# First head pair of a causal attention: score matmuls over 128 rows, with zero rows below the queries, keys and sums

## The chip, the core and the metric

The kernel runs on one core of one Trainium2 chip, in one launch. The metric is the device time of that core in microseconds (us). A single profiled execution gives the rows below; the times of separate runs stand in the table further down.

## The reference, cut to what matters

Attention over 4 batches, 8 heads, 576 positions and a head size of 64, with a bias from running sums, feeds two feed-forward layers. Only the scores of the attention matter here:

```python
scores = scale * np.matmul(q, k.transpose(0, 1, 3, 2))
cum = np.cumsum(np.maximum(s, 0.0), axis=-1)
bias = -(cum[:, :, :, None] - cum[:, :, None, :])
scores = np.where(causal, -1000000000.0, scores + np.minimum(bias, 0.0))
scores = scores - np.max(scores, axis=-1, keepdims=True)
attn = np.exp(scores)
attn = attn / (np.sum(attn, axis=-1, keepdims=True) + 1e-09)
```

The running sum of the key's position is added to the score; the part of the bias that depends on the query alone drops out of the softmax.

## The kernel before, in words

TensorE makes all products. The attention works on head pairs, 16 in all; each head has five chunks of 128 queries (the last has 64). For a chunk, TensorE makes the scores (`ps_s`, L766), VectorE subtracts them from a mask and takes the row minimum (L781), ScalarE takes the exponent (L789), TensorE turns the result in pieces of 128 columns (`pt`, L811), ScalarE copies it out of PSUM (L354), and TensorE multiplies it with the values (`px`, L842 in the first batch). The last chunk's scores come in two pieces of 288 columns.

The order of each engine's instructions is fixed when the program is built: a small planner (`Flow`) hands engines to generators by rank and its own estimates of cost, and the program is emitted in that order. Meanwhile the feed-forward weights are decoded: a 512 KB block `raw` is loaded, ScalarE squares a half of it (L386), VectorE works on it (L388, L394, L399, L404), then it is split into two parts (L331, L335). The buffer of `raw` is free for the next load when L404 has read it. All loads are issued by SyncE's queue in its own fixed order (L308), and a load that waits holds up all behind it.

The first head pair (batch 0, pair 0) is made in another way than the other 15. Its queries and keys stay in plain float32, loaded straight into the tiles `qf` and `kf` (`qt`, `kt` in the profile) of `first_qk`, which are made in `setup` (L510 to L515). They have 128 partitions and 576 columns, of which 64 partitions hold data. For the first head (j = 0) there are two score passes (`first_head`, L586 to L595): queries against keys over 64 rows, and a column of the identity against the 32 rows of running sums (`c8`, `c` in the profile). For the second head (j = 1) there is one pass over 65 rows: `copy(first_qk[1][1][D:D + 1], c8[1:2])` at L566 writes the running sum of that head into row 64 of `kf`, and row 64 of `qf` is set to one at L514. The other 15 pairs use passes of 128 and of 66 rows at L766.

Ahead of all this, `setup` has TensorE multiply the identity by itself 20 times (`warm`, L527, two matmul records for each), while the first loads are under way.

The trace writes a matmul's stationary tile as rows*columns: "64*128 64x256" contracts over 64 rows, has 128 stationary columns and streams 256 columns. A float32 matmul shows as two records ("x2").

Of the kernel before, what the change touches and what calls it, by code (L numbers as in the profile page):

```python
# [20 lines left out]
B, H, S, D = 4, 8, 576, 64  # L21
# [235 lines left out]
def attn_moe_moe2(ctx, tc, q, k, v, s, w_in, w_out, w1, w2, w3, w_out2, out):  # L257
    nc = tc.nc
    vec, act, pool, pe, sp = nc.vector, nc.scalar, nc.gpsimd, nc.tensor, nc.sync
# [32 lines left out]
    ident = const.tile([P, P], F32, name="ident")  # L292
# [210 lines left out]
    def setup():  # L503
        make_identity(nc, ident)
        pool.memset(above, 0.0)
        pool.affine_select(
            out=above[:, 4 * P:], in_=above[:, 4 * P:], pattern=[[-1, P]],
            compare_op=ALU.is_ge, fill=MASK, base=0, channel_multiplier=1,
        )
        for x in range(2):  # L510
            qf, kf = (
                ap.tile([P, S], F32, tag=f"{t}{x}", name=t, bufs=1) for t in ("qt", "kt")
            )
            pool.memset(qf[D:D + 1], 1.0)  # L514
            first_qk.append((qf, kf))  # L515
        vec.memset(half, 0.5)
        for z in range(3):
            sums_of[z] = ap.tile([P, 2 * NCH], F32, tag=f"sums{z}", name="sums", bufs=1)
            vec.memset(sums_of[z], 1.0)
        e4 = ap.tile([P, NCH * P], F32, name="e4", bufs=1)  # L520
        pool.memset(e4[:S - 4 * P, S:], 0.0)
        et[0, "e4"] = e4
        et[0, 0] = ap.tile([P, 2, 2, 256], F32, tag="e1", name="e1p", bufs=1)
        et[0, 1] = ap.tile([P, 2, NCH, 320], F32, tag="e2", name="e2p", bufs=1)
        warm = psa.tile([P, P], F32, tag="t0", name="warm", bufs=1)
        for n in range(WARM):
            pe.matmul(warm, lhsT=ident, rhs=ident, start=(n == 0), stop=(n == WARM - 1))  # L527
# [58 lines left out]
    def first_head(h, j, qf, kf, dq, dk):  # L586
        yield dq
        yield dk
        c8 = yield first_cum[j]
        if j == 0:  # L590
            h.ready.set([
                (qf[0:D], kf[0:D]), (ident[0:B * H, 0:1].to_broadcast([B * H, S]), c8),
            ])
        else:
            h.ready.set([(qf[0:D + 1], kf[0:D + 1])])  # L595

    def lend_decoder():
        for f in range(NA):
# [23 lines left out]
    def prepare(x):  # L622
        b, p = pairs[x]
        pr = pair[b, p]
        if x == 0:
            for j in range(2):
                r = slice(j * D, (j + 1) * D)
                h = heads[b, p, j]
                qf, kf = first_qk[j]
                dq = yield from load(qf[0:D], q[b, p][r], 4 * D * S)  # L630
                dk = yield from load(kf[0:D], k[b, p][r], 4 * D * S)
                h.release = [(QK, (yield QK.get()))]
                flow.start(flow.cur.prio, first_head(h, j, qf, kf, dq, dk))
            loaded[b, p].set()
            flow.start(flow.cur.prio, values_in(b, p))
            return
# [959 lines left out]
    def late_weights():  # L1596
        yield heads[WO_AFTER].ready
        for f in range(NA):
            flow.start(WO_PRIO + WO_STEP * f, decode(w_out[f], W, ("o", f)))

    setup()
    flow.start(-20, cumulate())
    flow.start(0, issue_pairs())
# [71 lines left out]
```

## Time and profile before

| | us |
|---|---|
| median of three runs | 930.67 |
| the runs | 930.1, 930.67, 937.26 |
| the profiled execution | 932.69 |
| its span, first to last instruction | 930.9 |

TensorE is busy for 912.9 us of the span, VectorE for 708.0, ScalarE for 480.6 and GpSimd for 191.6. The span lies 1.8 us under the profiled execution's own time. The granted clock of TensorE is given as a share of full speed: 1.00 is 2.4 GHz and 0.50 is 1.2 GHz; its mean over the span is 0.981.

### The profile page before, as it was taken

The page shows a single profiled execution, that of the slowest core. Times are in us where ns is not written, and L with a number is a line of the kernel's source. Part 1 is how long each engine was busy: PE and PEld are TensorE (multiplying, and loading weights), DVE is VectorE, ACT ScalarE, POOL GpSimd, SP SyncE. Part 2 cuts the span into 40 slices and gives each one's busy share as a digit, 9 for nine tenths or more (in the row PEclk, how much of TensorE's full clock was granted, in tenths as well). Part 3 has the DMA queues.
Part 4 walks back from the last instruction along what each step waited for, and adds up shares of the span by engine and source line. Part 5 has one row for each costly group of instructions (what it writes and reads, how often), then busy time and mean ns, then how long its engine had stood idle before and what let it go on. Part 6 is the DMA issues. An engine that isn't in the chain of part 4 may idle for free.

```text
span 930.9 us, 18684 instructions
## 1 busy us (share of the span) xinstructions
PE 912.9 (98%) x6532; PEld 856.4 (92%) x6532; DVE 708.0 (76%) x1816; ACT 480.6 (52%) x1216; POOL 191.6 (21%) x242
## 2 busy tenths in 40 slices
PE   9989799999999999999999999999999999999998
PEld 5545599999999999999999999999999999999998
DVE  5658978787878629998685899985858576677994
ACT  3667667787777635564453455543323232333552
POOL 4546865546543123300000000000000000000000
PEclk7899899999999999999999999999999999999999
DMA  6799977688776145664658587948752120283542
GB/s 185 195 258 252 256 220 208 178 244 229 200 199 177 48 150 167 219 206 145 192 183 299 168 302 262 347 178 323 243 184 65 63 66 33 85 300 103 165 142 77
DMA packets 97269, 174.93 MB, mean 188 GB/s; under 512 B 10620, under 2 KB 59772, under 8 KB 97176
## 3 DMA queue, kind: packets, MB, share of 16 engines
q1 hardware_dynamic: 97176, 173.75, 60.9%
q8 instruction: 52, 0.85, 0.4%
q14 instruction: 41, 0.34, 0.1%
HBM read 97.99 MB, written 49.17 MB: 158 GB/s over the span
## 4 chain that ended last, share of the span: by engine, by line
PE 84%; DVE 7%; DMA 5%; issue 1%; ACT 1%; SPq 1%; POOL 0%; DVEq 0%; POOLq 0%; ACTq 0%
PE ps_s L766 7%; PE ps_j L433 7%; PE ps_j L434 7%; PE ps_j L435 7%; PE ps_h L433 6%; PE ps_x L433 6%; PE ps_x L435 6%; PE ps_x L434 6%; PE ps_h L434 6%; PE ps_h L435 6%; PE pt L811 5%; PE px L849 5%; PE ps_o L434 2%; PE ps_o L435 2%; PE ps_o L433 2%; PE px L842 2%
## 5 line engine op out<-in xcount | busy, mean ns | idle before, releaser
L433 PE MATMUL ps_h<-x,w 128*128 128x288 f32 x512 | 155.3, 303 | 0.0
L433 PE MATMUL ps_x<-gt,w 128*128 128x288 f32 x512 | 153.0, 299 | 1.2 <-DVE g L978 1.2
L434 PE MATMUL ps_h<-x,w 128*128 128x288 f32 x512 | 151.2, 295 | 0.0
L435 PE MATMUL ps_x<-gt,w 128*128 128x288 f32 x512 | 151.2, 295 | 0.0
L435 PE MATMUL ps_h<-x,w 128*128 128x288 f32 x512 | 150.7, 294 | 0.0
L434 PE MATMUL ps_x<-gt,w 128*128 128x288 f32 x512 | 150.5, 294 | 0.2 <-DVE gt L335 0.2
L434 PE MATMUL ps_j<-xf,wf 128*128 128x288 f32 x432 | 127.9, 296 | 0.0
L433 PE MATMUL ps_j<-xf,wf 128*128 128x288 f32 x432 | 127.8, 296 | 0.0
L435 PE MATMUL ps_j<-xf,wf 128*128 128x288 f32 x432 | 127.6, 295 | 0.0
L974 ACT ACTIVATE u<-ps_h,half 128x288 f32<-128x288 f32 x128 | 63.9, 499 | 98.0 <-PE ps_h L435 97.6
L789 ACT ACTIVATE e<-e,tiny 128x128 f32<-128x128 f32 (+4 forms) x160 | 95.9, 600 | 27.5 <-DVE tiny L781 26.3
L766 PE MATMUL ps_s<-kt,qt 128*64 128x288 f32 (+13 forms) x384 | 99.5, 357 | 4.4 <-DVE tiny L781 1.6
L433 PEld LDWEIGHTS ps_x<-gt,w 128*128 128x128 f32 x512 | 96.2, 188 | 2.2 <-DVE g L978 1.7
L781 DVE CUSTOM_DVE_ANT_0 e<-ps_s,above 128x128 f32<-128x128 f32 (+4 forms) x160 | 75.5, 476 | 29.6 <-PE ps_s L766 28.4
L433 PEld LDWEIGHTS ps_h<-x,w 128*128 128x128 f32 x512 | 96.3, 188 | 0.9
L434 PEld LDWEIGHTS ps_x<-gt,w 128*128 128x128 f32 x512 | 96.3, 188 | 0.6 <-DVE gt L335 0.4
L434 PEld LDWEIGHTS ps_h<-x,w 128*128 128x128 f32 x512 | 96.5, 189 | 0.1
L435 PEld LDWEIGHTS ps_h<-x,w 128*128 128x128 f32 x512 | 96.3, 188 | 0.0
L435 PEld LDWEIGHTS ps_x<-gt,w 128*128 128x128 f32 x512 | 96.2, 188 | 0.0
L978 DVE SCALAR_TENSOR_TENSOR g<-u,ps_h 128x288 f32<-128x288 f32 x128 | 57.6, 450 | 41.6 <-ACT u L974 40.2
L329 ACT ACTIVATE gt<-g 128x288 fp32r<-128x288 f32 x128 | 56.5, 442 | 50.4 <-DVE g L978 50.1
L434 PEld LDWEIGHTS ps_j<-xf,wf 128*128 128x128 f32 x432 | 81.4, 188 | 0.0
(156 smaller groups left out, 2102.2 us busy)
## 6 DMA issues: line engine op xcount, KB each, us to landing
x<-x_d SPq DMA_DIRECT2D x64, 288.0 KB
f_d<-wf SPq DMA_DIRECT2D x30, 512.0 KB
wf<-f_d SPq DMA_DIRECT2D x30, 512.0 KB
kt<-kb SPq DMA_DIRECT2D x90, 144.0 KB
raw<-in_w_out_dram SPq DMA_DIRECT2D x22, 512.0 KB
x_d<-xs SPq DMA_DIRECT2D x16, 576.0 KB
raw<-in_w_dram SPq DMA_DIRECT2D x18, 512.0 KB
qt<-qb SPq DMA_DIRECT2D x30, 288.0 KB
```

Of the source, the lines that this page charges most:

```text
L329: act.activation(dst, src, AF.Copy)
L433: pe.matmul(ps, lhsT=wh, rhs=xh, start=first, stop=False, skip_group_check=again)
L434: pe.matmul(ps, lhsT=wh, rhs=xl, start=False, stop=False, skip_group_check=again)
L435: pe.matmul(ps, lhsT=wl, rhs=xh, start=False, stop=last, skip_group_check=again)
L766: pe.matmul(o, lhsT=lhs[:, qs], rhs=rhs[:, lo:hi], start=(x == 0), stop=(x == len(passes) - 1),)
L781: vec.tensor_tensor_reduce(out=e[:n, lo:hi], in0=ps[:n, 0:hi - lo], in1=above[:n, shift + lo:shift + hi], scale=-0.125, scalar=m0, op0=ALU ...
L789: act.activation(e[:n, :w], e[:n, :w], AF.Exp, bias=m0, scale=-1.0, accum_out=r,)
L811: pe.transpose(pt[:, y, :], e[:n, y * P:(y + 1) * P], ident[:n, :n])
L842: pe.matmul(px[0:D, z:n], lhsT=vhl[:, x, j], rhs=src[:, y, x, z:n], start=(x == 0), stop=last,)
L849: pe.matmul(px[:, z:n], lhsT=vhl[:, x, j].rearrange("p l d -> p (l d)"), rhs=src[:, hl, x, z:n], start=(x + hl == 0), stop=(last and hl == 1),
L974: act.activation(ut, ps, AF.Relu, bias=half, scale=1.0 / 6.0)
L978: vec.scalar_tensor_tensor(out=g, in0=ut, scalar=1.0, in1=ps, op0=ALU.min, op1=ALU.mult)
```

## The change

Both operand tiles of the first pair get defined values in all rows from 64 on: ones in `qf` (64 rows where there was one), zeros in `kf`. The scores of the two heads then contract over all 128 rows. Row 64 of the second head's `kf` is written later, with the running sum, by the same copy as before; the rows of zeros add nothing to a score. The 32-row pass over the running sums of the first head stays.

```diff
             qf, kf = (
                 ap.tile([P, S], F32, tag=f"{t}{x}", name=t, bufs=1) for t in ("qt", "kt")
             )
-            pool.memset(qf[D:D + 1], 1.0)
+            pool.memset(qf[D:], 1.0)
+            vec.memset(kf[D:], 0.0)
             first_qk.append((qf, kf))
...
         if j == 0:
             h.ready.set([
-                (qf[0:D], kf[0:D]), (ident[0:B * H, 0:1].to_broadcast([B * H, S]), c8),
+                (qf, kf), (ident[0:B * H, 0:1].to_broadcast([B * H, S]), c8),
             ])
         else:
-            h.ready.set([(qf[0:D + 1], kf[0:D + 1])])
+            h.ready.set([(qf, kf)])
```

The line numbers behind L514 grow by one. The order of instructions on TensorE, ScalarE and SyncE's queue stays as it was. VectorE's list begins like this before (`c_216` is the tile of running sums, `sp_t` the loaded input):

```order
L1670 UNCONDITIONAL_BRANCH
L516 MEMSET half 128x1
L519 MEMSET sums 128x10 x3
L552 TENSOR_SCALAR sp_t<-sp_t 32x576
L554 SCALAR_TENSOR_TENSOR cm<-sp_t 32x576
L559 TENSOR_SCALAR c_216<-cm 32x576
L331 CAST ch<-c_216 32x576
```

And like this now:

```order
L1671 UNCONDITIONAL_BRANCH
L515 MEMSET kt 64x576 x2
L517 MEMSET half 128x1
L520 MEMSET sums 128x10 x3
L553 TENSOR_SCALAR sp_t<-sp_t 32x576
L555 SCALAR_TENSOR_TENSOR cm<-sp_t 32x576
L560 TENSOR_SCALAR c_218<-cm 32x576
```

Two memsets stand at the front; nothing else moved. GpSimd's list around the memsets of `qf`, before:

```order
L505 MEMSET above 128x640
L506 AFFINE_SELECT above<-above 128x128
L514 MEMSET qt 1x576 x2
L521 MEMSET e_186 64x64
L335 TENSOR_TENSOR ch<-c_216,ch 32x576
```

And now:

```order
L505 MEMSET above 128x640
L506 AFFINE_SELECT above<-above 128x128
L514 MEMSET qt 64x576 x2
L522 MEMSET e_188 64x64
L335 TENSOR_TENSOR ch<-c_218,ch 32x576
```

The two memsets have 64 partitions where they had one, at the same place.

## Rows read from the trace of the kernel before

**Rows 1.** The page: the granted clock in 40 slices of the span, in tenths.
```profile
PEclk7899899999999999999999999999999999999999
```

**Rows 2.** Stretches of the span: busy time and instructions of each engine, clock, DMA.
```profile
core 0: us, PE busy (x) PEld busy (x) DVE busy (x) ACT busy (x) POOL busy (x), PEclk, DMA share, GB/s
...
7.50:11.40 3.90, 3.90 (x15) 1.86 (x13) 2.37 (x7) 2.33 (x6) 0.53 (x1) 1.00 1.03 287
11.50:31.90 20.40, 20.40 (x48) 9.36 (x48) 10.47 (x28) 10.85 (x28) 9.05 (x12) 0.50 0.50 155
...
45.00:59.00 14.00, 11.37 (x59) 5.90 (x57) 10.24 (x32) 9.74 (x26) 7.74 (x10) 1.00 1.05 240
59.30:62.60 3.30, 3.30 (x11) 2.10 (x11) 0.43 (x2) 2.15 (x6) 0.68 (x2) 0.50 1.04 347
...
100.00:121.00 21.00, 16.70 (x87) 14.19 (x87) 18.78 (x54) 13.77 (x39) 17.56 (x22) 0.76 0.88 229
...
121.00:929.00 808.00, 802.17 (x6021) 788.17 (x6020) 620.63 (x1571) 404.59 (x1016) 121.29 (x150) 1.00 0.58 182
```

**Rows 3.** TensorE in order of time: start us, busy us, line, tiles.
```profile
1.35 6.27 PE L527 MATMUL warm<-ident 128*128 128x128 f32 x40 [1.35 <-POOL ident masks.py:199]
...
9.00 0.69 PE L766 MATMUL ps_s<-c,ident 32*128 32x256 f32 x2
9.63 0.91 PE L766 MATMUL ps_s<-kt,qt 64*128 64x384 f32 x2
10.47 0.91 PE L766 MATMUL ps_s<-c,ident 32*128 32x384 f32 x2
...
11.62 2.07 PE L766 MATMUL ps_s<-kt,qt 64*128 64x512 f32 x2
13.62 2.07 PE L766 MATMUL ps_s<-c,ident 32*128 32x512 f32 x2
15.62 1.33 PE L811 MATMUL pt<-ident,e 128*128 128x128 f32 x5
16.88 1.22 PE L766 MATMUL ps_s<-kt,qt 64*64 64x288 f32 x2
18.03 1.22 PE L766 MATMUL ps_s<-c,ident 32*64 32x288 f32 x2
19.18 2.93 PE L766 MATMUL ps_s<-kt,qt 65*128 65x128 f32 x6
...
32.27 0.66 PE L811 MATMUL pt<-ident,e 128*128 128x128 f32 x4
32.86 0.70 PE L766 MATMUL ps_s<-kt,qt 65*64 65x288 f32 x2
33.40 0.70 PE L842 MATMUL px<-e2p,vf 128*64 128x320 f32 x2
```

**Rows 4.** Two stretches in which the DMA engines idle, same columns as rows 2.
```profile
16.30:22.30 6.00, 6.00 (x16) 3.05 (x15) 3.39 (x11) 3.70 (x10) 4.79 (x6) 0.50 0.00 1
28.90:32.20 3.30, 3.30 (x13) 1.76 (x11) 2.19 (x5) 2.29 (x6) 0.00 (x0) 0.54 0.04 9
```

**Rows 5.** VectorE, ScalarE and SyncE's queue in order of time: two weight loads.
```profile
12.64 9.64 SPq L308 DMA_DIRECT2D raw<-in_w_in_dram  x2
...
21.21 0.69 DVE L404 SCALAR_TENSOR_TENSOR da<-raw,da 128x512 uint32<-128x512 uint32 x1
...
25.87 0.66 ACT L386 ACTIVATE dm<-raw 128x512 f32<-128x512 f32 x1
...
31.45 0.69 DVE L404 SCALAR_TENSOR_TENSOR da<-raw,da 128x512 uint32<-128x512 uint32 x1
```

**Rows 6.** VectorE and GpSimd at the start, in order of time.
```profile
3.70 0.45 DVE L552 TENSOR_SCALAR sp_t<-sp_t 32x576 f32<-32x576 f32 x1 [2.74 <-DMA sp_t<-in_s_dram]
4.18 1.35 DVE L554 TENSOR_TENSOR_SCAN cm<-sp_t 32x576 f32<-32x576 f32 x1
2.29 1.09 POOL L514 MEMSET qt<- 1x576 f32 x2
```

## The prediction, made before the run

> **What bounds the kernel now.** I read the clock row of the page first. TensorE's granted clock falls short of full in the first two slices of 40 and in a few short later stretches, and is full for the rest [rows 1]. The table by stretches then says where time can be won. From 121 to 929 us TensorE is busy for 802 of 808 us at full clock [rows 2]: the back of the kernel is bound by TensorE and gets no shorter, but whatever starts it sooner ends it sooner. So only the front counts. There, from 11.5 to 31.9, TensorE is busy for all of 20.40 us, at half clock (0.50, that is 1.2 GHz), while VectorE and ScalarE are busy for about half of it [rows 2]. This is the one long stretch where TensorE is both the bound and slow.
>
> Why is it slow? It was not idle before: from 7.5 to 11.4 it was busy for 3.90 of 3.90 us at full clock, and then the clock fell [rows 2]. What it did then is in the order of time: after the warm-up products over 128 rows, passes that contract over 64 rows take turns with passes over 32 [rows 3]. From 45 to 59, where passes over 128 and 66 rows and value products over 128 fill TensorE, it is busy for only 11.37 of 14.00 us and the clock holds at 1.00 [rows 2]. Busier and slowed, idler and not: what differs is the rows in use. All score passes from 7.5 to 33.4 have 64, 32 or 65 rows. The warm-up bears on the zeros: it multiplies an identity, almost all zeros, and the steps after it run at full clock [rows 3]. So rows of zeros should count as rows.
>
> **The change part by part.** *Wider passes.* Rows cost no time: at full clock a 256-column pass over 32 rows takes 0.63 us from its start to the next start (9.00 to 9.63) and the 384-column pass over 64 rows 0.84 (9.63 to 10.47), and the 32-row one after it 0.83 up to the next piece of work [rows 3]; the price goes by columns. At half clock, 288 columns take 1.15 over 64 rows and 1.15 over 32 (16.88, 18.03, 19.18). I cost the widening itself at nothing.
>
> *The clock.* If it holds, the same work goes at the full-clock steps. 288 columns: 1.15 at half, 0.54 at full (32.86 to 33.40), ratio 0.47. 512 columns: 2.00 at half (11.62 to 13.62); at full, 0.63 and 0.84 give about 0.21 for every 128 columns, so 1.05, ratio 0.53. Transposes: 1.26 for five at half (15.62 to 16.88), 0.59 for four at full (32.27 to 32.86), 0.25 against 0.15 each, ratio 0.59 [rows 3]. Score passes make up most of the stretch, so I take 0.55 for all of it. TensorE alone would need 20.40 x 0.55 = 11.2 us and save 9.2; the ratios bound that at 8.4 and 10.8.
>
> It will not get all of this. VectorE has 10.47 us and ScalarE 10.85 us of work in the stretch [rows 2]; in 11.2 us they would be busy for 93% and 97%, and TensorE waits for both, since each chunk goes through minimum, exponent and copy. The weight loads wait too. SyncE's queue stands at two loads of `raw` from 12.64 to 22.28, the second until L404 (at 21.21) has read its buffer, and the DMA engines idle from 16.3 to 22.3 (share 0.00) and from 28.9 to 32.2 (0.04), in the second case until the next L404 at 31.45 [rows 4, 5]. Those L404 stand in VectorE's fixed order behind minima that wait for scores. I follow this chain. From 11.62 to 19.18, 7.56 us of TensorE's time become 4.2, so the second head's passes start 3.4 us sooner, and with them the L404 of 21.21. The load behind it is done no later than L386 at 25.87, which is 3.6 us from the end of its issue [rows 5]; that price stays. From L386 to the L404 of 31.45 lie 5.58 us, in which VectorE waits for TensorE: at 0.55 they become 3.1, another 2.5. By this chain the loads run 5.9 us sooner. So the stretch gains between 5.9 and 9.2 us; I take **6.6**, near the chain, because the other engines' 93 and 97% forbid the upper end.
>
> *What becomes of it up to 121 us.* From 45 on the loads bind with shares of 1.05 and 1.04, and TensorE idles 2.6 us from 45 to 59 and 4.3 from 100 to 121 [rows 2]. A faster TensorE alone would only wait longer there. But the queue restarts with L404, and the two idle stretches of DMA, 9.3 us together, shrink by about what the chain gains. Loads and TensorE thus move together, and I carry the 6.6 on unchanged. Late next are the exponents on ScalarE and the loads themselves.
>
> *The memsets.* GpSimd's two memsets of `qt` took 1.09 us for one partition of 576 columns each, and one of 128 partitions and 640 columns 0.63 [rows 6]. So 64 partitions cost 0.55 to 0.63 each, at most 0.2 us more together. They end near 3.5 us; the first score pass starts after 7.5. VectorE's two new memsets are not in the trace: the nearest rows of 576 columns are 0.45 (L552) and 1.35 (L554) [rows 6], so 0.9 to 2.7 us for both. I take 1.0, as L552 also does one plain step per column. They stand ahead of L552, before which VectorE idles for 2.74 us: even the upper end is covered. The first score pass now also waits for these memsets and holds all of TensorE behind it, but they are over some 4 us earlier. Without that cover the price would be at most 2.9 us, through the running sums. The copy of the running sum into row 64 must follow VectorE's memset, but the sums themselves come later from the same engine. All together: 0.
>
> **The sum.** In the profiled execution: 932.69 - 6.6 = 926.1 us, the 1.8 us around its span unchanged. Its own time stands 2.0 above the median of 930.67, so for a median I say 930.67 - 6.6 = **924.1 us**, 0.7% less.
>
> The Trainium skill, "TensorE: Matmul & The Clock Gate" (Part 1, the HAM clock gate), says that the gate follows how busy the PE has been lately, and names idle gaps as what brings it down; rows of the contraction are not in its rule. By that the change would give 930.7. The trace disagrees: TensorE busy for 3.90 of 3.90 us was followed by half clock, and 20.40 of 20.40 us did not lift it [rows 2].
>
> **The rivals.**
>
> *The clock falls all the same, but comes back sooner.* For it: in the first head half of the score columns still run over 32 rows, against none in the stretch from 45. Then only the second head's passes, over 128 rows throughout, lift the clock, say from 21.5 on. Of the 20.4 us about 10 would be gained back at a saving of 0.45, 4.5 us, less what the load chain keeps: 3.5. That gives 927.2 us.
>
> *Nothing changes, since zeros don't count.* Against it are the identity products of the warm-up; for it, that these have one nonzero value in each row and column, and the new moving rows have none. Then the stretch stays at 0.50 from 11.5 to 31.9 and the time at 930.7 us. It is also what the rule about busy time gives.
>
> *Slower: more cold stretches behind.* Loads bind from 45 to 121, and TensorE's clock already fell there, as at 59.3 to 62.6 (0.50) and for a part of 100 to 121 (mean 0.76) [rows 2]. TensorE finishes the first pair sooner, so it could stand idle for longer before the loads and be slowed where it now is not. A stretch as that of 59.3 holds 3.3 us at half clock and costs at most half of that, 1.6. If the loads gave back all 6.6, the first such stretch would make it slower than before, and six of them, 930.7 + 9.6 = 940.3, by over 1%. Against it: the loads themselves restart sooner, which narrows the idle time.
>
> **How the numbers follow.** Forecast 0.62, sooner return of the clock 0.18, nothing 0.12, slower 0.08. One per cent, 9.3 us, is about what a measurement of this kernel can tell from no change. The forecast at its upper ends (10.8 of TensorE alone, or 6.6 with two later cold stretches gone) passes it, in 0.15 of all cases; slower by over 1% takes 0.05, most of the last rival; the rest, 0.80, lies within 1%. The range goes from 919.5 (11.2 us gained: the upper ratio and a little from a later stretch) to 930.0: it takes in the forecast's 5.9 to 9.2, the sooner return, and stops short of the cases without gain.
>
> **What would show it.** Right: clock 1.00 from 11.5 on; the 512-column passes 1.05 us apart instead of 2.00; the second head's first pass near 15.8 instead of 19.18; the first DMA gap of 6.0 us shrunk to about 2.5; L404 of 31.45 near 24.8. Wrong: 0.50 in the same stretch with 128 rows shown (zeros don't count); full clock but VectorE or ScalarE idle for loads, with L404 late (the chain was mis-sized); a front that is 6 us ahead at 33 and no longer so at 121 (the loads or new cold stretches took it back).

## The result, and the profile after

The changed kernel took 926.06 us in the median of 18 runs (922.94 to 932.34), the kernel before 933.44 us in its 18 runs beside it (930.1 to 940.51). The ratio is 0.9917, with a 95% interval of 0.9896 to 0.9938: 0.83% less, or 7.7 us (7.4 us between the medians). The forecast was 6.6 us less (0.7%), at 924.1 us, with a range of 919.5 to 930.0. It stood on a median of three runs, 930.67; the 18 runs put the kernel before at 933.44, so the difference is the better thing to compare.

One word on the title, since the argument turns on rows: in the changed kernel only the keys have rows of zeros. The rows below the queries hold ones, and the sums' pass keeps its 32 rows.

The profiled execution of the changed kernel took 930.81 us, its span 929.0: it is the second slowest of the 18, and its mean clock over the span, 0.983, the second lowest. Its front shows the gain, and what lies behind 33 us shows how a part of it can be lost again; both are read below.

The stretches of the changed kernel, with the columns of [rows 2] and the same bounds:

```profile
7.50:11.40 3.90, 3.90 (x23) 2.45 (x21) 1.64 (x6) 1.07 (x4) 0.61 (x1) 1.00 1.04 329
11.50:31.90 20.40, 19.37 (x90) 10.31 (x91) 19.45 (x47) 15.49 (x43) 16.48 (x18) 1.00 0.75 203
45.00:59.00 14.00, 14.00 (x65) 7.55 (x63) 8.93 (x30) 10.13 (x28) 6.48 (x9) 0.90 0.89 225
59.30:62.60 3.30, 3.30 (x22) 1.94 (x21) 1.47 (x5) 2.43 (x8) 1.56 (x3) 1.00 1.06 266
100.00:121.00 21.00, 19.15 (x87) 16.28 (x86) 16.92 (x49) 12.03 (x32) 16.25 (x19) 0.61 0.85 232
121.00:929.00 808.00, 800.44 (x6011) 787.05 (x6010) 619.54 (x1568) 403.75 (x1014) 119.89 (x149) 1.00 0.58 182
```

From 11.5 to 31.9 the clock is 1.00 where it was 0.50, and TensorE gets 90 instructions done where it had 48 [rows 2]. VectorE is now busy for 19.45 of 20.40 us, as full as TensorE with 19.37. From 100 to 121 the mean clock is lower than before, 0.61 against 0.76.

TensorE in order of time, for the pieces of [rows 3]; line numbers are one higher:

```profile
1.35 7.38 PE L528 MATMUL warm<-ident 128*128 128x128 f32 x40 [1.35 <-POOL ident masks.py:199]
8.57 0.39 PE L767 MATMUL ps_s<-kt,qt 128*128 128x128 f32 x2
...
9.93 0.69 PE L767 MATMUL ps_s<-c,ident 32*128 32x256 f32 x2
10.55 0.91 PE L767 MATMUL ps_s<-kt,qt 128*128 128x384 f32 x2
...
12.40 1.02 PE L767 MATMUL ps_s<-kt,qt 128*128 128x512 f32 x2
13.35 1.12 PE L767 MATMUL ps_s<-c,ident 32*128 32x512 f32 x2
14.40 0.77 PE L812 MATMUL pt<-ident,e 128*128 128x128 f32 x5
...
16.35 1.57 PE L767 MATMUL ps_s<-kt,qt 128*128 128x128 f32 x6
```

The 512-column passes start 0.95 and 1.05 us apart from the next piece, against 2.00. The same 40 warm-up records took 7.38 us instead of 6.27, so the scores began at 8.57 us; still the second head's passes came at 16.35 instead of 19.18. The first scores of the kernel before, and the same two pieces of a second profile of the changed kernel (described below):

```profile
7.55 0.49 PE L766 MATMUL ps_s<-kt,qt 64*128 64x128 f32 x2
```

```profile
7.44 0.39 PE L767 MATMUL ps_s<-kt,qt 128*128 128x128 f32 x2
...
15.22 1.57 PE L767 MATMUL ps_s<-kt,qt 128*128 128x128 f32 x6
```

The start varies from execution to execution, and the 7.78 us between the first scores and the second head are the same in both. Before, they were 11.63 us.

The weight loads' chain of [rows 5], from VectorE, ScalarE and SyncE's queue:

```profile
13.57 5.79 SPq L308 DMA_DIRECT2D raw<-in_w_in_dram  x2
...
17.66 1.32 DVE L404 SCALAR_TENSOR_TENSOR da<-raw,da 128x512 uint32<-128x512 uint32 x1
...
20.26 0.67 ACT L386 ACTIVATE dm<-raw 128x512 f32<-128x512 f32 x1
...
24.60 1.18 DVE L404 SCALAR_TENSOR_TENSOR da<-raw,da 128x512 uint32<-128x512 uint32 x1
```

The L404 of 31.45 us comes at 24.60, 6.85 us sooner. Since the start varies, it is better counted from the first scores: 23.90 us before, 16.03 now, so 7.87 us less. The idle stretch of the DMA engines that lasted from 16.3 to 22.3 [rows 4] is now 2.4 us long, a row of stretches with the DMA share next to last:

```profile
17.00:19.40 2.40, 2.40 (x12) 1.15 (x10) 2.31 (x9) 1.98 (x6) 2.40 (x3) 1.00 0.00 0
```

### The profile page after: what moved, and what is told of

Same layout as the page of the kernel before. It is cut to its first block, busy times and chain, and to the rows that moved or that the text cites. A ratio compares the mean times of both kernels' runs of the same rounds, so it can differ in the third digit from the quotient of the medians.

```text
span 929.0 us, 18687 instructions
## 1 busy us (share of the span) xinstructions
PE 910.6 (98%) x6532; PEld 857.4 (92%) x6532; DVE 710.8 (77%) x1818; ACT 479.6 (52%) x1216; POOL 193.2 (21%) x242
## 4 chain that ended last, share of the span: by engine, by line
PE 84%; DMA 6%; DVE 6%; issue 1%; SPq 1%; ACT 1%; POOL 0%; DVEq 0%; POOLq 0%; ACTq 0%
PE ps_j L433 7%; PE ps_j L434 7%; PE ps_j L435 7%; PE ps_h L433 7%; PE ps_x L433 7%; PE ps_x L435 6%; PE ps_x L434 6%; PE ps_h L434 6%; PE ps_h L435 6%; PE ps_s L767 6%; PE px L850 5%; PE pt L812 4%; DMA raw<-in_w_in_dram 3%; PE ps_o L434 2%; DMA kt<-kb 2%; PE ps_o L435 2%
## 5 line engine op out<-in xcount | busy, mean ns | idle before, releaser
L767 PE MATMUL ps_s<-kt,qt 128*64 128x288 f32 (+9 forms) x384 | 97.5, 352 | 4.0 <-DMA kt<-kb 3.3
```

The source lines that it names most:

```text
L767: pe.matmul(o, lhsT=lhs[:, qs], rhs=rhs[:, lo:hi], start=(x == 0), stop=(x == len(passes) - 1),)
```

## Experiments: which rows, and whose

Theory A at this point: the clock held because more rows of the array were in use. The first four runs take the change apart. Each ratio is against the kernel before on the same chip.

**The memsets alone.** Both memsets stay wide, the passes go back to 64 and 65 rows:

```diff
-                (qf, kf), (ident[0:B * H, 0:1].to_broadcast([B * H, S]), c8),
+                (qf[0:D], kf[0:D]), (ident[0:B * H, 0:1].to_broadcast([B * H, S]), c8),
...
-            h.ready.set([(qf, kf)])
+            h.ready.set([(qf[0:D + 1], kf[0:D + 1])])
```

> The wide memsets of the change stay, the score passes of the first pair contract over 64 and 65 rows again. Theory A (the rows of the contraction hold the clock): granted clock 0.50 from about 11.5 to about 32 us as before, the L404 that stood at 31.45 us within 1 us of it, time within 0.3% of before. Rival B (the rows don't matter; the longer memsets shift the start, or the clock was luck): clock 1.00 in that stretch and the time near 0.992 of before.

Measured: 0.9997 (0.9976 to 1.0017), L404 at 31.40 us. The stretch in which the clock was low, same columns as above:

```profile
12.60:29.60 17.00, 17.00 (x39) 7.50 (x37) 8.01 (x22) 9.16 (x24) 9.06 (x12) 0.50 0.50 149
```

TensorE is busy without a gap and stays at half clock. The memsets show no gain and no cost; Rival B falls. The mean clock over the span, which is on record for every execution, agrees: 0.974 to 0.985 in the 12 of this run, 0.972 to 0.987 in 51 of the kernel before, and 0.987 to 0.994 in 16 of the change's 18.

**The first head alone.** The second of the two lines above goes back to 65 rows, the first stays wide.

> Only the first head's passes contract over 128 rows, the second head's over 65 again. Theory A: the clock holds past 11.5 us, through the first head's passes, to about 16 us or later; the second head's passes over 65 rows may let it fall for some us between 16 and 30. L404 of 31.45 us comes 3 to 7 us sooner, time 0.993 to 0.998 of before. Rival B (rows don't matter): clock and time as before.

Measured: 0.9910 (0.9886 to 0.9933), L404 at 23.79 us. The stretch as above:

```profile
11.50:31.90 20.40, 19.45 (x91) 10.28 (x91) 19.60 (x49) 15.41 (x43) 17.10 (x19) 1.00 0.77 220
```

All of the gain comes with the first head: from the first scores at 7.76 us, L404 took 16.03 us, as in the change. That the second head's 65 rows might let the clock fall was a miss: they held it at 1.00.

**The second head alone.** The first line goes back to 64 rows, the second stays wide.

> Only the second head's passes contract over 128 rows; the first head's have 64 and 32 rows as before. Theory A: the clock falls near 11.5 us as before and comes back between 21 and 26 us instead of 32; L404 of 31.45 us comes 2 to 4 us sooner, time 0.995 to 0.998 of before. Rival B: clock and time as before, 0.50 up to 32 us.

Measured: 0.9978 (0.9955 to 1.0001), L404 at 30.63 us. The clock fell, and came back between the two expectations:

```profile
11.10:28.00 16.90, 16.90 (x37) 7.43 (x36) 8.04 (x24) 8.28 (x23) 9.07 (x12) 0.50 0.56 181
28.10:40.00 11.90, 11.66 (x62) 6.71 (x60) 11.06 (x31) 9.29 (x26) 7.27 (x8) 1.00 0.66 162
```

It rose at 28 us, not at 21 to 26 nor at 32, and L404 came 0.8 us sooner, not 2 to 4; the time fits Theory A's upper end and no change alike. This profile is of the execution with the lowest mean clock of the 12 (0.977, the others up to 0.991), so the rise may come sooner in others. Nor do the second head's passes stand alone: the first head's last 288 columns, over 64 and 32 rows, come between them, from 22.8 to 25.1 us. What can be said is that the same passes went with either clock. The second head's 65-row passes ran at 1.00 in the run with the first head alone wide, which met them at full clock, and at 0.50 until 29.6 us with the memsets alone, which met them at half clock. (The first head's pieces between them differ, 128 and 32 rows against 64 and 32.)

**96 rows.** Both heads' passes take `qf[0:96]` and `kf[0:96]`.

> Both heads' passes contract over 96 rows (32 zero rows for the first head, 31 for the second) instead of 128. Theory A (rows are what counts, by degrees): the clock falls during the first head, whose other half has 32 rows, and comes back in the second head; between before and the change: L404 of 31.45 us 1 to 5 us sooner, time 0.994 to 0.999. Rival C (any rows beyond 64 or 65 are enough, as whole rows are either used or not): as the change, clock 1.00 from 11.5 to 32 us and time 0.992 of before.

Measured: 0.9938 (0.9914 to 0.9962), L404 at 23.96 us (16.03 from the first scores), clock 1.00 from 11.5 to 31.9. In the front it does all that 128 rows do, against what Theory A was expected to show, and as Rival C had it: anything beyond 64 rows. The time lies between, but its interval holds the change's ratio too. The next runs settle Rival C.

## Experiments: the running sums' pass

**The sums' pass over 128 rows, the rest as before.** The tile of sums gets 128 rows, zeroed first, and the identity's column all its rows:

```diff
-        c8 = make(z, [B * H, S], F32, "c8")
+        c8f = make(z, [P, S], F32, "c8")
+        vec.memset(c8f, 0.0)
+        c8 = c8f[0:B * H]
...
-        first_cum[0].set(c8)
+        first_cum[0].set(c8f)
...
-                (qf[0:D], kf[0:D]), (ident[0:B * H, 0:1].to_broadcast([B * H, S]), c8),
+                (qf[0:D], kf[0:D]), (ident[:, 0:1].to_broadcast([P, S]), c8),
```

> The kernel before, but the running sums' pass of the first head contracts over 128 rows instead of 32 (their tile is zeroed first); queries against keys stay at 64 rows, the second head at 65. Theory A (rows in use count, whichever pass has them): the first head then has 64 and 128 rows in turn, more than the 128 and 32 of the change, so the clock holds from 11.5 to 32 us at 1.00, L404 of 31.45 us comes 6 to 8 us sooner and the time is 0.990 to 0.994 of before. Rival D (it is the queries against keys themselves that must fill the rows): 0.50 from 11.5 us on as before, and the time within 0.3% of before.

Measured: 0.9920 (0.9898 to 0.9943), L404 at 24.02 us, mean clock 0.93 from 11.5 to 31.9 (low only from 29.1 to 32.5). The queries against keys have 64 rows as before, and the gain is that of the change: it doesn't matter which pass brings the rows. Rival D falls.

**The change with the sums' pass over 128 rows too.** The same edit on the changed kernel.

> The change, with the running sums' pass over 128 rows too. Theory A with a clock that already holds: nothing more to gain in the first pair, time 0.990 to 0.993 of before as with the change. Rival E (in some executions of the change the clock still falls in the first head, whose sums have 32 rows): one or two tenths of a per cent better than the change, 0.988 to 0.990.

Measured: 0.9892 (0.9871 to 0.9913). L404 came at 21.80 us, 2.80 us ahead of the changed kernel's, which neither theory had. A part of that is an earlier start; counted from the first scores (7.50 us) it took 14.30 us, against 16.03. TensorE in order of time tells where the 1.7 us come from:

```profile
7.94 0.60 PE L769 MATMUL ps_s<-kt,qt 128*128 128x256 f32 x2
8.38 0.59 PE L769 MATMUL ps_s<-c,ident 128*128 128x256 f32 x2
8.81 0.81 PE L769 MATMUL ps_s<-kt,qt 128*128 128x384 f32 x2
9.46 0.81 PE L769 MATMUL ps_s<-c,ident 128*128 128x384 f32 x2
10.10 0.27 PE L814 MATMUL pt<-ident,e 128*128 128x128 f32 x1
```

From start to start a 256-column pass takes 0.43 to 0.44 us and one of 384 columns 0.64 to 0.65, at the same full clock at which the kernel before and the changed one take 0.62 to 0.63 and 0.83 to 0.84. Two weight loads show what the 0.19 us are, of this kernel first, then of the changed one:

```profile
8.16 0.41 PEld L769 LDWEIGHTS ps_s<-c,ident 128*128 128x128 f32 x2
```

```profile
10.55 0.30 PEld L767 LDWEIGHTS ps_s<-kt,qt 128*128 128x128 f32 x2 [0.33 <-issue]
```

With equal rows the weights of the next pass load while a pass still streams (8.16, before 8.38). Where 128 rows follow 32, the load starts only with the end of the pass before (10.55, behind the pass that began at 9.93; 0.33 us of idle time stand before it). Theory F: passes with different numbers of rows wait for their weights. The Trainium skill, "TensorE: Matmul & The Clock Gate" (Part 2, step ①), says that a weight load is pulled ahead where row groups don't conflict or where it goes to a background buffer; these rows agree that it can be, and show the case in which it is not.

**64 rows throughout.** To part rows from waits, on the kernel before the sums' pass gets 64 rows, as the queries against keys have. The edit is that of the first run of this section, with `c8f[0:D]` and `ident[0:D, 0:1].to_broadcast([D, S])`.

> The kernel before, but the running sums' pass contracts over 64 rows instead of 32, as the queries against keys do; nothing has 128 rows. Theory F (a pass whose rows differ in number from those of the pass before waits for its weights, 0.19 us at full clock): the steps from pass to pass in the first head at full clock are 0.43 us for 256 columns and 0.65 for 384, against 0.63 and 0.84. Theory A (rows in use count over time): 64 rows throughout, with no gaps, are about as much as the 96 and 32 that held the clock, so the clock holds or falls late, L404 of 31.45 us comes 5 to 9 us sooner and the time is 0.989 to 0.995 of before. Rival C (only passes over more than 64 rows hold the clock): 0.50 from about 11 us on, time 0.997 to 1.000.

Measured: 0.9911 (0.9888 to 0.9935), L404 at 23.11 us, TensorE in order of time:

```profile
9.20 0.59 PE L768 MATMUL ps_s<-kt,qt 64*128 64x256 f32 x2
9.63 0.59 PE L768 MATMUL ps_s<-c,ident 64*128 64x256 f32 x2
10.06 0.81 PE L768 MATMUL ps_s<-kt,qt 64*128 64x384 f32 x2
10.71 0.81 PE L768 MATMUL ps_s<-c,ident 64*128 64x384 f32 x2
```

```profile
11.50:31.90 20.40, 18.95 (x90) 10.56 (x90) 19.68 (x48) 15.51 (x43) 17.00 (x19) 0.97 0.82 227
```

Both theories hold. The steps are 0.43 and 0.65 us, so equal rows do it, not 128 of them; and the clock holds to 30.8 us with no score pass of the first head over more than 64 rows, so Rival C falls. What the kernel before lacked was only in its 32-row passes: they used a quarter of the rows, and made TensorE wait at each turn. This run mends both at once, so which of the two holds the clock here is not shown. In the change the waits stayed (0.62 and 0.84 us a step), so there it was the rows.

**The values of the added rows.** Ones in the moving operand, zeros in the stationary one:

```diff
-            pool.memset(qf[D:], 1.0)
-            vec.memset(kf[D:], 0.0)
+            pool.memset(qf[D:], 0.0)
+            if x == 1:
+                pool.memset(qf[D:D + 1], 1.0)
+            vec.memset(kf[D:], 1.0)
```

> The change with the parts exchanged: the added rows of the moving operand hold ones, those of the stationary one zeros (row 64 of the second head apart, which one more memset of 0.55 us on GpSimd sets). If zeros in the moving rows weaken what the rows do for the clock: fewer cold stretches and 0.1 to 0.3% under the change. If the values don't count: clock 1.00 from 11.5 to 32 us and the time of the change, 0.990 to 0.993.

Measured: 0.9939 (0.9917 to 0.9961), L404 at 24.87 us, clock 1.00 from 11.5 to 31.9. From the first scores to L404 it took 16.03 us once more, and the median, 927.86 us, is near that of the change beside it on one chip (927.1, below). Moving ones do no more than moving zeros.

## Experiments: what is lost behind the front

How far the changed kernel is ahead can be read from one instruction of VectorE in both traces, as its order is the same. Two such places, the kernel before first, then the changed one:

```profile
50.37 0.50 DVE L781 CUSTOM_DVE_ANT_0 e<-ps_s,above,tiny 64x288 f32<-64x288 f32 x1
...
125.54 0.92 DVE L331 CAST w<-da 128x512 fp32r<-128x512 f32 x1
```

```profile
47.37 0.50 DVE L782 CUSTOM_DVE_ANT_0 e<-ps_s,above,tiny 64x288 f32<-64x288 f32 x1
...
124.14 0.92 DVE L331 CAST w<-da 128x512 fp32r<-128x512 f32 x1
```

The lead is 6.85 us at L404, 3.00 at the first of these and 1.40 at the second, where the long part begins that TensorE bounds. With the first head alone wide, the same front kept its lead, 7.66 us at L404, 8.02 and 6.56 here:

```profile
42.35 0.50 DVE L782 CUSTOM_DVE_ANT_0 e<-ps_s,above,tiny 64x288 f32<-64x288 f32 x1
...
118.98 0.92 DVE L331 CAST w<-da 128x512 fp32r<-128x512 f32 x1
```

The stretches say where it went, two of the changed kernel, then the second of them in the kernel before and with the first head alone wide:

```profile
33.00:37.50 4.50, 2.61 (x16) 1.66 (x17) 2.59 (x8) 2.36 (x7) 0.52 (x1) 1.00 1.08 224
37.70:47.80 10.10, 10.10 (x34) 5.59 (x33) 5.16 (x14) 5.14 (x16) 1.42 (x2) 0.50 1.05 202
```

```profile
37.70:47.80 10.10, 8.99 (x49) 5.41 (x49) 7.88 (x25) 7.85 (x23) 3.29 (x5) 1.00 1.01 231
```

```profile
37.70:47.80 10.10, 10.08 (x53) 5.43 (x52) 8.25 (x24) 8.13 (x21) 6.15 (x7) 1.00 1.06 247
```

TensorE, sooner done with the first pair, stands before the load of the next (1.9 us at one pass, by the table of waits), is then at half clock for 10.1 us and gets 34 instructions done. In the kernel before it was busy for all 4.50 us of the first stretch, and did 49 in the second, at full clock; with the first head alone wide it was busy for 3.22 us of the first, with a longest wait of 1.3 us, and did 53 in the second, also at full clock. So this is a matter of each execution. How often a loss of this size comes can be read from the mean clock over the span: two of the 18 executions of the changed kernel have 0.979 and 0.983 and took 932.34 and 930.81 us, the second of them the profiled one. The other 16 have 0.987 to 0.994 and took 922.94 to 928.75 us.

**The change once more**, beside others on one chip.

> The changed kernel itself, beside the other three on one chip: 0.990 to 0.993 of before, with L404 of 31.45 us 6 to 8 us sooner.

Measured: 0.9931 (0.9904 to 0.9957), L404 at 23.47 us, 7.98 us sooner than before and again 16.03 us from the first scores. Its profile, once more of an execution with the second lowest mean clock (0.980, at 931.65 us; the median of the 12 is 927.1), has the same loss, after 2 us without any work on TensorE:

```profile
33.00:35.00 2.00, 0.00 (x0) 0.00 (x0) 0.53 (x2) 0.89 (x3) 0.00 (x0) 1.00 1.01 248
35.40:48.90 13.50, 13.50 (x44) 7.58 (x43) 6.21 (x19) 6.33 (x18) 1.41 (x2) 0.50 1.03 204
```

The lead at the two places of VectorE is 2.70 and 0.48 us here.

**More rows in the other pairs.** The 66-row passes of the other 15 pairs go over 128 rows, in the hope that they keep the clock up behind such waits:

```diff
-                pool.memset(qt.bitcast(F32)[D:D + 2, 0], 1.0)
+                pool.memset(qt.bitcast(F32)[D:, 0], 1.0)
+                pool.memset(kt.bitcast(F32)[D:, 0], 0.0)
...
-                (qt[:, 1], kt[:, 1]), (qt[0:D + 2, 0], kt[0:D + 2, 0]),
+                (qt[:, 1], kt[:, 1]), (qt[:, 0], kt[:, 0]),
```

> The change, and the 66-row passes of the other 15 pairs contract over 128 rows as well (zeros below row 65; a second memset of 0.57 us on GpSimd for each of three slots). If the cold stretches between 33 and 121 us are what takes the gain back (in the changed kernel's profile 30.7 us at half clock, gain 6.9 us at 31 us and 1.5 us at 121 us): fewer of them, time 0.984 to 0.989 of before. If they only fall where TensorE waits for loads anyway: time as the change, 0.990 to 0.994, with cold stretches left that begin after idle TensorE.

Measured: 0.9910 (0.9887 to 0.9932), as the change. The mean clock from 32 to 121 us was 0.95 in its profile, against 0.83 and 0.79 in the two of the change; but these two have low mean clocks among their like, and it was 0.92 in the kernel before and with 96 rows. Three cold stretches were left, near 31, 45 and 106 us, and over whole spans the mean clock, 0.990 to 0.994, is as in most executions of the change. No gain beyond the change's shows.

**All score passes over 128 rows**, both edits on the changed kernel.

> The change with all score passes over 128 rows, the running sums' pass and the 66-row passes of the other pairs. If both rivals hold that speak for more rows, 0.982 to 0.988 of before; if rows are enough already and loads bind the rest, 0.990 to 0.994, as the change.

Measured: 0.9899 (0.9879 to 0.9919). With the sums' pass alone it was 0.9892, so the other pairs' rows bring nothing that shows. Passes over 128 rows throughout do not keep the clock up behind a wait: in this profile TensorE stood for 2.2 us before the keys of the next pair, at 27.4 us, and the clock was 0.50 from 27.5 to 34.

**The sums' pass over 128 rows, again**, beside the change on one chip.

> The change with the running sums' pass over 128 rows, again. Theory F: all passes of the first head have the same number of rows, steps 0.44 and 0.65 us for 256 and 384 columns, L404 of 31.45 us 9 to 10 us sooner, time 0.2 to 0.3% under that of the change in the same call (0.988 to 0.990). If the difference between the calls was the chip: as the change.

Measured: 0.9913 (0.9890 to 0.9937), L404 at 22.77 us, 8.7 us sooner instead of 9 to 10; counted from the first scores it took 14.07 us, 9.8 less than before. The steps are those of the first time, and the median is 1.7 us under the change's (925.45 and 927.1), but the intervals overlap both times: that this version beats the changed kernel is likely by its front and not shown by its time.

## Why the prediction was right, and where it was not

**The clock, right.** That rows in use and not busy time set it apart is shown: by the memsets alone (TensorE busy for 17.00 of 17.00 us at half clock), the first head alone, and the sums' pass alone. The change leaves the steps from pass to pass as they were, at 0.62 to 0.63 and 0.84 us, so only its rows can hold the clock. The rule about busy time of the Trainium skill, "TensorE: Matmul & The Clock Gate" (Part 1, the HAM clock gate), would have left the time as it was; the measured 0.9917 differs. It need not be 128 rows, though: 64 in every pass are enough, where the gap of 0.19 us that 32-row passes open at each turn is gone too. The prediction did not see this gap, and the trace counts it as busy time.

**The widening costs nothing: right as a price, too narrow as a step.** It read 0.63 and 0.84 us as prices by columns. Of these 0.19 us each are a wait for weights that equal rows take away (0.44 and 0.65). The change itself keeps that wait, with 128 after 32 rows.

**The chain of loads: the right path, sized too small, and near the mark by luck.** L404 came at 24.60 us; the forecast was 31.45 - 6.6 = 24.85. But the scores began 1.02 us late in this profile. Counted from the first scores, the L404 came 7.87 us sooner, where the chain added up to 5.9 and the pick was 6.6. Term by term, counted in the same way: the L404 of 21.21 came 4.57 us sooner (13.66 to 9.09 us), forecast 3.4, and TensorE's second head 3.85 (11.63 to 7.78). The second term, the price of 3.6 us from the end of the issue to L386, did not stay. L386 followed 0.9 us behind (13.57 + 5.79 = 19.36, then 20.26), as its load was the first of the two that were issued there and had landed by 17.0, where the DMA engines fall idle; so L386 came 6.63 us sooner. The third gave back less than it was put at: from L386 to L404 it took 4.34 us where 3.1 was forecast, with VectorE busy for 95% of the stretch from 11.5 us, as the working feared of the other engines. VectorE's own steps had grown there, L399 for one, before and now:

```profile
30.72 0.69 DVE L399 SCALAR_TENSOR_TENSOR da<-dm,da 128x512 uint32<-128x512 uint32 x1
```

```profile
23.46 1.10 DVE L399 SCALAR_TENSOR_TENSOR da<-dm,da 128x512 uint32<-128x512 uint32 x1
```

GpSimd stood idle beside the first of them and worked beside the second; that this is the cause was not tested.

**The memsets: right.** VectorE's two took 1.15 us (estimate 1.0), before its wait for the running sums' input, and GpSimd's two took 1.09 us as before [rows 6]:

```profile
0.91 1.15 DVE L515 MEMSET kt<- 64x576 f32 x2 [0.91 <-PEq L1658]
...
2.29 1.09 POOL L514 MEMSET qt<- 64x576 f32 x2
```

The wider memset of 0.63 us, from which the working took its upper price, is not among [rows 6]; it is this row of the kernel before:

```profile
1.24 0.63 POOL L505 MEMSET above<- 128x640 f32 x1
```

**Carrying 6.6 us on unchanged: right for the median, wrong for single executions.** The step said that loads and TensorE move together. By the medians 7.4 of the front's 7.9 us arrive. In both profiles of the change, each with the second lowest mean clock of its kind, TensorE came to the loads of the next pairs too soon, and the lead shrank to 3.00 and 2.70 us near 50 and to 1.40 and 0.48 near 125. That is the mechanism of the third rival, at a price of 3.9 us up to the first place for a longer wait and 10.1 us at half clock; with the first head alone wide, a wait of 1.3 us without the half clock cost nothing there.

**The other rivals.** The second falls (zeros count as ones do). The first, an earlier return of the clock, is what the second head alone shows, at 0.9978; that is 2.1 us, and the interval, from no gain to 4.2 us, takes in its 3.5.

## What to carry to other kernels

Where TensorE is busy without a gap and yet at half clock, look at the rows that its passes contract over and at the steps from pass to pass, not at its busy time; filling rows with zeros costs a memset that idle engines can take. Give passes that take turns the same number of rows: that alone, with 64 rows and none of the change's zeros in the keys, had the same time here. And follow such a gain to the next stretch that waits for loads: an engine that arrives there sooner can go cold and lose what it brought. Look at which execution was profiled, too: both profiles of the change have a low mean clock for this kernel, and what they lose is not what the median loses.

## What the runs showed of the hardware that was not expected

Weights for a pass over as many rows as the one before loaded beside it; between 128 and 32, 96 and 32, 64 and 32, or 64 and 128 rows they did not, at 0.19 us a turn at full clock. Between 65 rows and transposes over 128 no such wait shows, in the run with the first head alone wide:

```profile
18.73 0.33 PE L812 MATMUL pt<-ident,e 128*128 128x128 f32 x1
18.90 1.02 PE L767 MATMUL ps_s<-kt,qt 65*128 65x512 f32 x2
19.76 0.71 PE L812 MATMUL pt<-ident,e 128*128 128x128 f32 x5
```

The 512 columns take 0.86 us from start to start, where 1.05 would hold a wait of 0.19; 96 rows in that place take 0.86 as well. So a different number of rows is not enough for the wait, and which pairs beyond these wait is open. The clock looked easier to hold than to regain: with 65-row passes in the second head it stayed at 1.00 when it came to them full, and at 0.50 until 29.6 us when it came to them low; with the first head's pieces between them not the same in the two runs, this is likely and not shown.
